# The second MLP product of three batches as seven half-width block products per pair of token blocks

## The chip, the cores and the metric

The kernel runs on one core of a Trainium2 chip. The metric is the device time of one execution in microseconds (us), as the median of several runs. One execution was also recorded by the hardware profiler; its records give the views that are quoted below. Engine names are those of the profile: PE is TensorE's matrix product, PEld its weight load, DVE is VectorE, ACT is ScalarE, POOL is GpSimd, SP is SyncE, which issues the DMAs.

## What is computed

Two blocks in a row, in float32. First an mLSTM cell over 4 batches, 8 heads, 768 time steps and a head size of 40 (a gated linear recurrence; the kernel computes it in chunks of 128 steps). Its output, brought to the shape (4, 768, 320), is `x` of the second block:

```python
X = np.fft.fft(np.fft.fft(x, axis=1), axis=2)
u = x + np.real(X)
un = (u - u.mean(-1)) / np.sqrt(u.var(-1) + 1e-06)
ch = np.maximum(un @ w_ch1, 0.0) @ w_ch2      # 320 -> 1280 -> 320
out = u + ch
```

The change concerns the last product, `relu(...) @ w_ch2`, and the sum with `u`.

## The kernel before

**Order of the work.** The order on every engine is written out by hand. `at(slot, phase, fn, ...)` (L113) puts a function into a plan, `run` (L116) calls all of them in order of slot and phase, and each engine executes its instructions in the order in which they were issued. Within a slot the phases are EVAC (0), FILL (1 and fractions), MAIN (2), FILL_PE (3 and more). MAIN holds the MLP products; FILL holds what DVE, ACT and POOL do for the mLSTM and the Fourier mix of the following batches; FILL_PE holds those batches' PE products, so they come between the MLP products of one slot and those of the next. An engine that waits keeps everything queued behind it waiting as well.

**Tiling.** Tokens come in six blocks of 128 a batch, in the order `ORDER` (L41): three form group 0, three group 1. The hidden features come in ten blocks of 128 (NFF, L27). Batch 0 starts its MLP in slot 31, batches 1, 2 and 3 in slots 63, 95 and 127 (L991 to L995). Each MLP has 20 slots for the first product and 12 for the second.

**First product, batches 1 to 3** (`mlp_block`, L871). Five blocks, each for two hidden feature blocks and both groups (384 tokens each), and each with four steps of one slot. It is already the seven-product scheme: the products accumulate in four PSUM banks p1, p2, p5 and p3, and p1 is read by ACT between two products (L907, L911, L916), so that the next product may add to it. At the end of step 3 DVE adds three banks to the copied values (L921 to L925 by way of L890), POOL applies negated relu to the three results (L893), and ACT takes the fourth straight out of p1 with relu (L927). The next block uses the four banks in reversed order.

**Second product** (`mlp_out`, L929). For each of the six token blocks ten matmuls of 320 columns accumulate in one bank, five in each of two slots (L934). One DVE instruction then multiplies by `rstd`, adds `u` and writes the tile `ot` (L940), and SP stores it (L942).

**Mix.** `mix_seq`, `mix_tail` and `mix_feat` (L636, L649, L700) are its PE products. `mix_add` (L720) adds the transform to `x`, writes the tile `u`, and takes mean and variance (L742, L743): six or eight DVE instructions a token block. `mix_center` (L745, ACT), `mix_turn` (L753, PE) and `mix_turn_out` (L760, ACT) turn it into the first product's operand `uT`. `mlp_sums` (L864) makes four sums of `uT` on DVE ahead of each first product. The mix of batch b+1 lies in the 12 slots of batch b's second product.

**PSUM.** The pool `ps_m` (L82) has four banks that all of these tiles take in rotation. A tile waits until the bank's last reader is done.

Of the kernel before, what the change touches and what calls it, by code (L numbers as in the profile page):

```python
# [19 lines left out]
L = 128  # L20
# [30 lines left out]
def kernel(  # L51
# [25 lines left out]
    xp = pool("xp", 2)  # L77
# [4 lines left out]
    ps_m = pool("ps_m", 4, space=PSUM)  # L82
# [22 lines left out]
    Cd_bufs = [const.tile([L, NP, D1], FP, name=f"Cd{n}") for n in range(2)]  # L105
# [19 lines left out]
    def idle_products(n, ps=ps_s, tag="ps"):  # L125
        pw = ps.tile([L, 2 * L], FP, name="pi", tag=tag)
        for i in range(n):
            nc.tensor.matmul(pw, rest[:, 0:L], rest, start=True, stop=True, skip_group_check=True)


    def gates(gp):
# [19 lines left out]
        idle_products(3, ps_m, "pm")  # L151
# [45 lines left out]
        def spread_max(b, c, h0):  # L197

            k = chunks[b, c]
            if h0 == 0:  # L200
                k.W = wp.tile([L, H, L], FP, name="W", tag="W")
                k.M = []
            k.M.append(ps_m.tile([L, NP, L], FP, name="pM", tag="pm"))
            nc.tensor.matmul(k.M[-1], ident_b, later_b.unsqueeze(1).to_broadcast([L, NP, L]), start=True, stop=False,
                             skip_group_check=True)
            for h in range(h0, h0 + NP):
                bh = b * H + h
                w, x = (ident[:, bh:bh + 1], M[:, c, :]) if c < 2 else (sel[:, bh:bh + 1], M3[:, c, :])
                nc.tensor.matmul(k.M[-1][:, h - h0, :], w.to_broadcast([w.shape[0], L]), x, start=False, stop=True,
                                 skip_group_check=True)  # L210
# [10 lines left out]
        def spread_decay(b, c):  # L221
            k = chunks[b, c]
            k.G = ps_m.tile([L, NP, L], FP, name="pG", tag="pm")
            for h in range(H):
                r, bh = slice(h % 2 * 64, (h % 2 + 1) * 64), b * H + h
                nc.tensor.matmul(k.G[r, h // 2, :], ident[:, bh:bh + 1].to_broadcast([L, 64]), g[:, c, :],
                                 start=True, stop=True)
# [54 lines left out]
        def decays():  # L282
# [4 lines left out]
            pd = ps_m.tile([L, BH // 2, NT - 1], FP, name="pd", tag="pm")  # L287
# [234 lines left out]
    def mlstm_turn(b, c, early):  # L522
        k = chunks[b, c]
        k.px = ps_m.tile([L, NP, L], FP, name="px", tag="pm") if early else ps_h.tile([L, NP, L], FP, name="px", tag="ph")
        for p in range(NP):
            nc.tensor.transpose(k.px[:, p, :], k.hT[:, p, :], ident)  # L526

    def mlstm_finish(b, c):

        k = chunks.pop((b, c))  # L530
        if c == 0:
            xs[b] = xp.tile([L, NT, DM], FP, name="x", tag="x")
# [8 lines left out]
        nc.vector.tensor_tensor(out=xs[b][:, c].rearrange("p (h d) -> p h d", d=D), in0=h1[:, :, 0:D], in1=sc,  # L541
# [41 lines left out]

    def copy(eng, out, in_):
        (nc.scalar.copy if eng == 0 else nc.vector.tensor_copy)(out=out, in_=in_)

    def mix_fold(b, p):
# [3 lines left out]
        x = xs[b]  # L591
# [44 lines left out]
    def mix_seq(b, p, parts):  # L636
# [3 lines left out]
        if p == TG - 1:  # L640
            k.pz = getattr(k, "pz", []) + [ps_m.tile([L, NK], FP, name="pz", tag="pm") for _ in parts]
# [7 lines left out]
    def mix_tail(b, p):  # L649

        k = mixes[b]
        if p == TG - 1:
            k.pzt = ps_m.tile([L, NK], FP, name="pzt", tag="pm")
# [46 lines left out]
    def mix_feat(b, p):  # L700
# [6 lines left out]
        pu = k.pu[p] = ps_m.tile([L, DM + 1 + NC], FP, name="pu", tag="pm")  # L707
# [12 lines left out]
    def mix_add(b, c):  # L720
# [3 lines left out]
        if c == ORDER[0]:  # L724
            k.u = u_p.tile([L, NT, DM + 2], FP, name="u", tag="u")
        ops = (OP.subtract, OP.add) if c >= NT // 2 else (OP.add, OP.subtract)
        u, x, n = k.u[:, c, 0:DM], xs[b][:, c], HALF_D - 1
        pu = k.pu[min(c, NT - 1 - c)]
        P, Q = pu[:, 0:NC], pu[:, NC:DM]
        if b == 0:  # L730
            nc.vector.tensor_tensor(out=u, in0=x, in1=pu[:, 0:DM] if c < TG else backwards(pu, DM, DM), op=OP.add)
        else:
            nc.vector.tensor_tensor(out=u[:, 0:NC], in0=x[:, 0:NC], in1=P, op=OP.add)
            nc.vector.tensor_tensor(out=u[:, NC:], in0=x[:, NC:], in1=backwards(P, n, n), op=OP.add)
            nc.vector.tensor_tensor(out=u[:, 1:HALF_D], in0=u[:, 1:HALF_D], in1=Q, op=ops[0])
            nc.vector.tensor_tensor(out=u[:, NC:], in0=u[:, NC:], in1=backwards(Q, n - 1, n), op=ops[1])
        if c == TG:
            r, own = slice(0, 1), pu[0:1, DM + 1:]
            nc.vector.tensor_tensor(out=u[r, 0:NC], in0=x[r, 0:NC], in1=own, op=OP.add)
            nc.vector.tensor_tensor(out=u[r, NC:], in0=x[r, NC:], in1=backwards(own, n, n), op=OP.add)  # L740
# [12 lines left out]
    def mix_turn(b, c):  # L753

        k = mixes[b]
        pt = k.pt[c] = ps_m.tile([L, 3, L], FP, name="put", tag="pm")
# [56 lines left out]
    def mlp_in(b, gr, f):  # L813
# [4 lines left out]
        if f % 2 == 0:  # L818
            k.pm = [ps_m.tile([L, TG * L], FP, name="pm", tag="pm") for _ in range(2)]
# [7 lines left out]

    def mlp_relu(b, gr, f):
        k = mixes[b]
        if f == 0:  # L830
            k.h[gr] = []
        ht = hT_p.tile([L, TG * L], FP, name="hT", tag="hT")
        nc.scalar.activation(out=ht, in_=k.pm[f % 2], func=AF.Relu, scale=-1.0)  # L833
        k.h[gr].append(ht)
# [36 lines left out]
    def mlp_block(b, i, step):  # L871
# [20 lines left out]
        def relu(h):  # L892
            nc.gpsimd.tensor_scalar(out=h, in0=h, scalar1=-1.0, scalar2=0.0, op0=OP.mult, op1=OP.max)  # L893

        if step == 0:
            if i == 0:
                k.h = {0: [], 1: []}
            banks = [ps_m.tile([L, TG * L], FP, name="pm", tag="pm") for _ in range(4)]
            k.pm = banks[::-1] if i % 2 else banks
            for gr, r in ((0, 0), (1, 0), (0, 1), (1, 1)):  # L900
                k.h[gr].append(hT_p.tile([L, TG * L], FP, name="hT", tag="hT"))
        p1, p2, p5, p3 = k.pm
        (h11, h21), (h12, h22) = k.h[0][f:], k.h[1][f:]
# [13 lines left out]
        else:  # L917
# [4 lines left out]
            relu(h12)  # L922
            add(h22, p5)
            relu(h22)
            add(h11, p2)  # L925
            relu(h11)
            nc.scalar.activation(out=h21, in_=p1, func=AF.Relu, scale=-1.0)  # L927

    def mlp_out(b, gr, i, half):  # L929
        k = mixes[b]  # L930
        if half == 0:
            k.po = ps_m.tile([L, DM], FP, name="po", tag="pm")
        for f in range(half * NFF // 2, (half + 1) * NFF // 2):
            nc.tensor.matmul(k.po, k.h[gr][f][:, i * L:(i + 1) * L], w2_sb[:, f, :], start=(f == 0), stop=(f == NFF - 1))  # L934

    def mlp_store(b, gr, i):
        k = mixes[b]
        c = ORDER[gr * TG + i]
        ot = ot_p.tile([L, DM], FP, name="ot", tag="ot")
        nc.vector.scalar_tensor_tensor(out=ot, in0=k.po, scalar=k.rstd[:, c:c + 1], in1=k.u[:, c, 0:DM],  # L940
                                       op0=OP.mult, op1=OP.add)
        nc.sync.dma_start(out=out[b, c * L:(c + 1) * L, :], in_=ot)  # L942
# [3 lines left out]
    def plan_mlp(b, s):  # L946
        groups = range(NT // TG)
        for i in range(NFF // 2) if b > 0 else ():
            for step in range(4):
                at(s, MAIN, mlp_block, b, i, step)  # L950
                s += 1
        for gr in groups if b == 0 else ():
# [6 lines left out]
        for gr in groups:  # L959
# [11 lines left out]
    def plan_batch(b, s_mlstm, s_mix, s_mlp):  # L971
# [9 lines left out]
        else:  # L981
            feat = [s_mix + 3, s_mix + 4, s_mix + 6]
            add = [s_mix + c for c in (4, 4, 5, 6, 7, 7)]
            turn = [s_mix + c for c in (5, 6, 6)]
            late = [s_mix + c for c in (7, 8, 8)]
# [10 lines left out]
    for n in range(4):  # L996
        at(s_mlp + 2 * NFF + 1 + n, FILL + 0.4, weight_sums, n)

# [26 lines left out]
    u_p = pool("u", 2)  # L1025
    st_p = pool("st", 2)
    hT_p = pool("hT", 2 * NFF)
    ot_p = pool("ot", 2)
# [102 lines left out]
```

## Time and profile before

| what | value |
|---|---|
| median of 3 runs (lowest, highest) | 437.33 us (436.42, 437.35) |
| the profiled execution's own time | 437.06 us |
| its span, first to last instruction | 435.4 us |
| PE busy | 419.1 us, 96% of the span |
| DVE, ACT, POOL busy | 251.6, 169.6, 164.7 us |
| TensorE clock granted | 0.999 |

The time outside the span is 1.7 us. PE's records overlap their neighbours[...]; the pitch from one start to the next is the time it holds the engine. A float32 matmul of the source gives two records in the profile, so 240 matmuls of L934 show as 480. In the groups, the columns are line, engine, operation, tiles (out<-in), shapes and number of records; then busy time in us and mean ns of one; then the idle time of the engine just before these records and what ended it.

Batch 1's second product lies at about 227 to 282 us of the span, batch 2's at 324 to 367 us, batch 3's at 400 to 432 us. Batch 3's has no other batch's work beside it.

### The profile page before, as it was taken

The page shows a single profiled execution, that of the slowest core. Times are in us where ns is not written, and L with a number is a line of the kernel's source. Part 1 is how long each engine was busy: PE and PEld are TensorE (multiplying, and loading weights), DVE is VectorE, ACT ScalarE, POOL GpSimd, SP SyncE. Part 2 cuts the span into 40 slices and gives each one's busy share as a digit, 9 for nine tenths or more (in the row PEclk, how much of TensorE's full clock was granted, in tenths as well). Part 3 has the DMA queues.
Part 4 walks back from the last instruction along what each step waited for, and adds up shares of the span by engine and source line. Part 5 has one row for each costly group of instructions (what it writes and reads, how often), then busy time and mean ns, then how long its engine had stood idle before and what let it go on. Part 6 is the DMA issues. An engine that isn't in the chain of part 4 may idle for free.

```text
span 435.4 us, 7369 instructions
## 1 busy us (share of the span) xinstructions
PE 419.1 (96%) x2696; PEld 284.5 (65%) x2696; DVE 251.6 (58%) x621; ACT 169.6 (39%) x448; POOL 164.7 (38%) x191
## 2 busy tenths in 40 slices
PE   8998999999999999979999999999999999999997
PEld 6877555666577777746457778765457776445774
DVE  8799867689977166587632546667731552343111
ACT  6976376666543114543242334453220131332000
POOL 6454111355424303156682320536681000567000
PEclk9999999999999999999999999999999999999999
DMA  7889396669445424078002334210000000000000
GB/s 245 259 242 336 106 266 221 207 185 280 141 130 160 138 75 150 1 217 206 2 0 87 108 125 131 88 32 3 0 0 17 15 30 32 0 1 2 30 30 30
DMA packets 20547, 47.11 MB, mean 108 GB/s; under 512 B 2784, under 2 KB 9312, under 8 KB 20384
## 3 DMA queue, kind: packets, MB, share of 16 engines
q1 hardware_dynamic: 20512, 46.65, 34.9%
q8 instruction: 21, 0.34, 0.3%
q14 instruction: 14, 0.11, 0.1%
HBM read 42.52 MB, written 4.11 MB: 107 GB/s over the span
## 4 chain that ended last, share of the span: by engine, by line
PE 75%; DVE 14%; DMA 3%; issue 3%; ACT 2%; POOL 1%; SPq 0%; DVEq 0%; POOLq 0%
PE po L934 30%; PE pm L881 13%; PE ps L456 5%; PE ph L477 4%; PE pm L886 3%; PE ph L470 3%; PE pu L718 3%; PE px L526 2%; DMA raw<-in_w 2%; PE pz L687 2%; PE put L758 2%; DMA kvt<-in_kv 1%; PE pz L675 1%; DVE W L462 1%; PE pc L487 1%
## 5 line engine op out<-in xcount | busy, mean ns | idle before, releaser
L934 PE MATMUL po<-w_sb,hT 128*128 128x320 f32 x480 | 135.2, 434 | 0.0
L934 PEld LDWEIGHTS po<-w_sb,hT 128*128 128x128 f32 x480 | 89.6, 190 | 36.9 <-issue 1.4
L893 POOL TENSOR_SCALAR hT<-hT 128x384 f32<-128x384 f32 x45 | 66.3, 1494 | 63.2 <-DVE hT L890 63.2
L434 POOL TENSOR_SCALAR_AFFINE_SELECT W<-W 128x1024 f32<-128x1024 f32 x18 | 21.0, 1166 | 85.3 <-ACT W L412 46.3
L890 DVE TENSOR_TENSOR hT<-hT,pm 128x384 f32<-128x384 f32 x60 | 30.5, 550 | 38.2 <-ACT hT L911 25.7
L940 DVE SCALAR_TENSOR_TENSOR ot<-po,rstd,u 128x320 f32<-128x320 f32 x24 | 13.2, 549 | 67.6 <-PE po L934 67.5
L412 ACT ACTIVATE W<-W,colT 128x128 f32<-128x128 f32 x144 | 45.1, 396 | 0.0
L881 PE MATMUL pm<-uT,w_sb 128*128 128x384 f32 x90 | 32.8, 493 | 3.4 <-DVE hT L890 3.3
L462 DVE TENSOR_TENSOR W<-ps,W 128x512 f32<-128x512 f32 x48 | 30.7, 680 | 7.3 <-POOL W L434 7.0
L822 PE MATMUL pm<-uT,w_sb 128*128 128x384 f32 x80 | 29.9, 500 | 1.1 <-ACT hT L833 0.6
L763 ACT COPY uT<-put 128x384 f32<-128x384 f32 x24 | 10.9, 479 | 48.0 <-PE put L758 48.0
L456 PE MATMUL ps<-qk 40*128 40x128 f32 x384 | 28.1, 284 | 0.0
L456 PEld LDWEIGHTS ps<-qk 40*128 40x128 f32 x384 | 23.7, 187 | 4.4 <-issue 1.0
L477 PE MATMUL ph<-W,kvt 128*41 128x128 f32 x384 | 25.8, 277 | 0.0
L881 PEld LDWEIGHTS pm<-uT,w_sb 128*128 128x128 f32 x90 | 16.0, 190 | 14.9 <-DVE hT L890 7.3
L422 POOL TENSOR_TENSOR qg<-qk,Gb 128x512 f32<-128x512 f32 x18 | 25.5, 1415 | 0.8 <-DMA qk<-in_qkT 0.7
L470 PEld LDWEIGHTS ph<-qg,C 128*128 128x128 f32 x160 | 20.2, 191 | 7.9 <-issue 4.2
L470 PE MATMUL ph<-qg,C 128*128 128x128 f32 x160 | 21.7, 279 | 2.6 <-DVE x L541 1.0
L886 PE MATMUL pm<-uT,w1t_sb 64*128 64x384 f32 x120 | 23.9, 509 | 0.0
L477 PEld LDWEIGHTS ph<-W,kvt 128*41 128x41 f32 x384 | 19.5, 117 | 3.0 <-DVE fe L602 0.2
L515 ACT COPY h<-ph 41x512 f32<-41x512 f32 (+1 forms) x16 | 9.3, 580 | 28.2 <-PE ph L477 28.1
L822 PEld LDWEIGHTS pm<-uT,w_sb 128*128 128x128 f32 x80 | 13.7, 189 | 9.8 <-issue 1.4
(187 smaller groups left out, 643.8 us busy)
## 6 DMA issues: line engine op xcount, KB each, us to landing
W<-M_d SPq DMA_DIRECT2D x18, 512.0 KB
kvt<-in_kv SPq DMA_DIRECT2D x24, 324.0 KB
qk<-in_qkT SPq DMA_DIRECT2D x48, 160.0 KB
raw<-in_w SPq DMA_DIRECT2D x10, 640.0 KB
Gb<-G_d SPq DMA_DIRECT2D x36, 128.0 KB
so<-in_o SPq DMA_DIRECT2D x24, 160.0 KB
out<-ot SPq DMA_DIRECT2D x24, 160.0 KB
ds_sb<-in_dft_s SPq DMA_DIRECT2D x1, 1155.0 KB
```

The source lines that it names most:

```text
L412: nc.scalar.activation(out=k.W[:, h, :], in_=M, func=AF.Exp, scale=-1.0, bias=colT[:, c, 0, b * H + h:b * H + h + 1])
L422: nc.gpsimd.tensor_tensor(out=k.qg, in0=k.qk[:, 0], in1=k.Gb, op=OP.mult)
L456: nc.tensor.matmul(k.ps[hip][:, p, :], k.qk[r, 1, p, :], k.qk[r, 0, p, :], start=True, stop=True)
L462: nc.vector.tensor_tensor(out=Wv, in0=k.ps[hip], in1=Wv, op=OP.mult)
L470: nc.tensor.matmul(k.ph[:, p, :], k.C[:, p, :], k.qg[:, p, :], start=(p == 0), stop=False, skip_group_check=True)
L477: nc.tensor.matmul(k.ph[hip * 64:hip * 64 + D1, p, :], k.v1[:, 2 * p + hip, :], k.W[:, 2 * p + hip, :], start=(c == 0 and p == 0), stop=Tr ...
L822: nc.tensor.matmul(k.pm[i], w1_sb[:, ch, f0:f0 + L], u[2 * ch], start=(ch == 0), stop=False)
L881: nc.tensor.matmul(bank, w, u, start=start, stop=True, skip_group_check=True)
L886: nc.tensor.matmul(bank, block(w1t_sb, i)[rows], mlp_u(gr, 1)[rows], start=False, stop=True, skip_group_check=True)
L890: nc.vector.tensor_tensor(out=h, in0=h, in1=bank, op=OP.add)
L893: nc.gpsimd.tensor_scalar(out=h, in0=h, scalar1=-1.0, scalar2=0.0, op0=OP.mult, op1=OP.max)
L934: nc.tensor.matmul(k.po, k.h[gr][f][:, i * L:(i + 1) * L], w2_sb[:, f, :], start=(f == 0), stop=(f == NFF - 1))
```

## The change

Batch 0 keeps its second product. Batches 1 to 3 get another one. One token block of group 1 and one of group 0 form a pair, the ten hidden blocks fall into five even and five odd ones, and the 320 output columns into two halves of 160. This is a 2 by 2 by 2 block product, and `mlp_out_pair` does it with seven block products of five matmuls of 160 columns, in four slots: two products in steps 0, 1 and 2, one in step 3. The two PSUM banks x and y are used in turns. After every block product one DVE instruction (`residual`) adds the bank's present content, times `rstd`, to one half of one token block of `u`; x then goes on accumulating on what was read.

The scheme needs sums of operands. Four sums of weights (`out_weight_sums`) are made once, on POOL. Four sums of hidden values (`hidden_sums`) are made for each pair. For pair 0 POOL makes them for four fifths of the features, two slots ahead of the end of the first product, and DVE makes the last fifth at the head of the first slot of the second product; for pairs 1 and 2 DVE makes S1 and S3 and POOL S2 and S4, in the two last slots of the pair before.

Further parts: the three relus of each first-product block go from POOL to ACT (`mlp_relus`), in EVAC of the slot after step 3. `u` is no longer a tile of its own: `mix_add` and `residual` work in place on `x`, which is kept in two fixed buffers, and the store reads from there. The PSUM pool has four tags of one bank. Where no bank is named they rotate as before; the pairs use banks 0 and 1, and the mix of batches 2 and 3 banks 2 and 3. Of the mix of batches 2 and 3, the third feature product, two adds and four turns come one or two slots later. A token block's store is issued in MAIN, right after its last `residual`, where it stood in EVAC of the next slot; and `mlstm_finish` (L528), which fills `x` of batch b+2, now waits for the stores of batch b.

```diff
-            nc.tensor.matmul(k.po, k.h[gr][f][:, i * L:(i + 1) * L], w2_sb[:, f, :], start=(f == 0), stop=(f == NFF - 1))
...
+    MIX = {"z": (2, 3), "zt": 2, "u": (3, 2, 2), "ut": (3, 3, 3, 3, 2, 3)}
...
-        def relu(h):
-            nc.gpsimd.tensor_scalar(out=h, in0=h, scalar1=-1.0, scalar2=0.0, op0=OP.mult, op1=OP.max)
...
+            k.pm = [bank("pm", [L, TG * L], n) for n in (range(4) if i % 2 else range(3, -1, -1))]
...
             add(h12, p3)
-            relu(h12)
             add(h22, p5)
-            relu(h22)
             add(h11, p2)
-            relu(h11)
             nc.scalar.activation(out=h21, in_=p1, func=AF.Relu, scale=-1.0)
 
+    def mlp_relus(i):
+        for gr, r in ((1, 1), (1, 0), (0, 0)):
+            h = hidden(gr, 2 * i + r)
+            nc.scalar.activation(out=h, in_=h, func=AF.Relu, scale=-1.0)
+
+    def residual(b, c, cols, po):
+        k = mixes[b]
+        u = k.u[:, c, cols]
+        nc.vector.scalar_tensor_tensor(out=u, in0=po, scalar=k.rstd[:, c:c + 1], in1=u, op0=OP.mult, op1=OP.add)
...
+    MLP_PAIRS = ((0, 1), (2, 0), (1, 2))
...
+    def out_weight_sums(n):
...
+        nc.gpsimd.tensor_tensor(out=o, in0=x, in1=y, op=OP.subtract)
...
+    def hidden_sums(eng, n, which, f0=0, f1=NFF // 2):
...
+        for j in which:
+            o, x, y, op = ((S1, A21, A22, OP.add), (S2, S1, A11, OP.subtract), (S3, A11, A21, OP.subtract),
+                           (S4, A12, S2, OP.subtract))[j - 1]
+            eng.tensor_tensor(out=o, in0=x, in1=y, op=op)
+
+    def mlp_out_pair(b, n, step):
...
+        if step == 0:
+            k.po = [bank("po", [L, HALF_D], (n + j) % 2) for j in range(2)]
...
+        def product(po, a, w, start=False):
+            for f in range(half):
+                nc.tensor.matmul(po, a[:, f], w[:, f], start=start and f == 0, stop=f == half - 1, skip_group_check=True)
...
+        if step == 0:
+            product(x, pair_block(n, 1, 1), w[0, 0], True)
+            residual(b, c1, first, x)
+            product(y, pair_block(n, 1, 0), w[1, 0], True)
+            residual(b, c1, first, y)
+        elif step == 1:
+            product(x, s(2), w2x["T2"])
+            residual(b, c1, last, x)
+            product(y, s(1), w[0, 1], True)
+            residual(b, c2, last, y)
+        elif step == 2:
+            product(x, s(3), w2x["T3"])
+            residual(b, c2, last, x)
+            product(y, s(4), w[1, 1])
+            residual(b, c1, last, y)
+            store(b, c1)
+        else:
+            product(x, pair_block(n, 0, 0), w2x["T4"])
+            residual(b, c2, first, x)
+            store(b, c2)
...
                 at(s, MAIN, mlp_block, b, i, step)
                 s += 1
+            at(s, EVAC, mlp_relus, i)
...
+        if b > 0:
+            at(s - 2, FILL + 0.3, hidden_sums, nc.gpsimd, 0, (1, 2, 3, 4), 0, NFF // 2 - 1)
+            at(s, EVAC, hidden_sums, nc.vector, 0, (1, 2, 3, 4), NFF // 2 - 1, NFF // 2)
+        for n in range(TG) if b > 0 else ():
+            for step in range(4):
+                at(s, MAIN, mlp_out_pair, b, n, step)
+                if n < TG - 1 and step > 1:
+                    for eng, j in ((nc.vector, 2 * step - 3), (nc.gpsimd, 2 * step - 2)):
+                        at(s, FILL + 0.3, hidden_sums, eng, n + 1, (j,))
+                s += 1
...
+            feat = [s_mix + c for c in ((3, 4, 6) if b == 1 else (3, 4, 7))]
+            add = [s_mix + c for c in ((4, 4, 5, 6, 7, 7) if b == 1 else (4, 4, 5, 6, 8, 8))]
+            turn = [s_mix + c for c in ((5, 6, 6) if b == 1 else (5, 6, 7))]
+            late = [s_mix + c for c in ((7, 8, 8) if b == 1 else (8, 9, 10))]
...
+        at(s_mlp + MLP_SLOTS + 3 + 3 * n, FILL + 0.4, out_weight_sums, n)
```

## The prediction, made before the changed kernel was run

> **What bounds the kernel now.** I read the page first: engine shares, then the chain that ended last.
>
> ```profile
> PE 419.1 (96%) x2696; PEld 284.5 (65%) x2696; DVE 251.6 (58%) x621; ACT 169.6 (39%) x448; POOL 164.7 (38%) x191
> PE 75%; DVE 14%; DMA 3%; issue 3%; ACT 2%; POOL 1%; SPq 0%; DVEq 0%; POOLq 0%
> ```
>
> PE is the bound, and three quarters of the chain are its own. Then the groups that the change touches, and the busy time by stage (batch 1's second product, batch 2's first, batch 2's second, batch 3's first, batch 3's second; columns: stretch, length, then busy us of PE, PEld, DVE, ACT, POOL).
>
> ```profile
> L934 PE MATMUL po<-w_sb,hT 128*128 128x320 f32 x480 | 135.2, 434 | 0.0
> L893 POOL TENSOR_SCALAR hT<-hT 128x384 f32<-128x384 f32 x45 | 66.3, 1494 | 63.2 <-DVE hT L890 63.2
> L940 DVE SCALAR_TENSOR_TENSOR ot<-po,rstd,u 128x320 f32<-128x320 f32 x24 | 13.2, 549 | 67.6 <-PE po L934 67.5
> ...
> 226.00:282.50 56.50, 56.50 (x406) 43.62 (x408) 26.49 (x74) 21.23 (x60) 20.08 (x24) 1.00 0.32 104
> 282.50:324.00 41.50, 39.85 (x231) 23.84 (x228) 27.03 (x78) 14.48 (x35) 24.01 (x25) 1.00 0.03 9
> 324.00:367.00 43.00, 43.00 (x190) 30.99 (x190) 16.30 (x50) 7.30 (x15) 4.26 (x3) 1.00 0.06 20
> 367.00:399.60 32.60, 32.50 (x112) 16.51 (x111) 12.35 (x34) 9.15 (x19) 18.22 (x13) 1.00 0.02 5
> ```
>
> In the second-product stages PE never rests and no other engine is busy half the time. So time saved on PE there is saved in full, unless a new wait appears. Where would one? Two places in the timeline. First, a boundary between two blocks of batch 3's first product (start, length, instruction, idle before it):
>
> ```profile
> 379.36 0.91 PE L881 MATMUL pm<-m,w_sb 128*128 128x384 f32 x2
> 380.11 2.10 PE L881 MATMUL pm<-uT,w_sb 128*128 128x384 f32 x6
> 382.05 0.81 PE L881 MATMUL pm<-raw 128*128 128x384 f32 x2
> ...
> 380.31 0.49 ACT L927 ACTIVATE hT<-pm 128x384 f32<-128x384 f32 x1 [1.84 <-PE pm L881]
> 381.01 0.48 ACT L907 COPY hT<-pm 128x384 f32<-128x384 f32 x1 [0.21 <-POOL hT L893]
> ```
>
> PE's new block starts at 380.11; the product at 382.05 adds to p1 and needs L907's copy, done at 381.49. ACT has 0.56 us to spare. Second, the pitch of narrow matmuls and DVE's lumps in batch 1's second product:
>
> ```profile
> 244.57 0.71 PE L718 MATMUL pu<-dd_sb,Z 128*128 128x161 f32 x4
> 245.12 0.70 PE L718 MATMUL pu<-dd_sb,Zt 128*128 128x320 f32 x2
> ...
> 245.86 0.32 DVE L733 TENSOR_TENSOR u<-x,pu 128x161 f32<-128x161 f32 x1 [0.53 <-PE pu L718]
> 249.17 1.27 DVE L462 TENSOR_TENSOR W<-ps,W 128x512 f32<-128x512 f32 x2
> ```
>
> Four records of about 160 columns take 245.12 - 244.57 = 0.55 us, 0.136 each (the same pair at 248.35 and 248.89 gives 0.135). From 245.86 DVE does two `mix_add` (3.3 us) and one weighing (1.27), 4.6 us without a break.
>
> [...] L934's pitch is 32.31 us for 120 records in the chain, 0.269 us[...]. For 160 it gives 0.136, as measured on L718; weight loads of 128 columns stay hidden at that pitch there. [...] L869 took 0.56 us alone and 1.32 beside POOL. [...]
>
> **What the change takes away.** Per batch, 120 records of 0.269 (32.3 us) become 3 pairs x 35 matmuls x 2 records = 210 of 0.136 (28.6 us). Over three batches: 96.9 - 85.7 = 11.2 us. The last residual is half as wide: 0.549 less 160 columns at the slope between L731 (320 columns, 0.474) and L733 (161, 0.309), so 0.38; it ends the kernel, 0.17 saved. Sum 11.4. POOL loses 45 relus, 66 us, off the path: no gain counted.
>
> **What it adds on the path.**
>
> *Relus on ACT.* Each is queued ahead of the next block's L907. Consecutive ACT instructions overlap by 0.10 (L412: 144 of 0.396 busy 45.1, a pitch of 0.313), so three take 3 x 0.42. From L927 at 380.31: relus start at 380.70, 381.12 and 381.54, L907 at 381.96, done 382.44. PE starts 0.06 later and its first weight load shows (0.1; such a record takes 0.42 instead of 0.32): 382.60 for 382.05, 0.55 us lost. Batch 3 has four such boundaries: 2.2. In batches 1 and 2 the first two are covered by another batch's product between the blocks or by PE's own wait for DVE, the third is late by about 0.4 (ACT waits there for DVE's adds, which end 0.9 us after PE's restart), the fourth has no cover: 0.95 a batch. Sum 4.1. Bounds: 0.48 a relu (L520, 320 columns) gives 3.2, 0.61 (L751, with a bias operand) gives 6.1. Exponentials queued behind the relus have a slot to spare.
>
> *Into the second product.* DVE's four last sums (128 elements, about 0.28 + wait, 1.3 us) wait for ACT's third relu, and the residual of x is queued behind them. In batch 3: relus end 2.1 us after PE's start, sums 3.4, residual 3.75, and PE wants x again at 2.72: 0.85 to 1.0, with 0.15 before it for the fifth matmul, which waits for a relu. In batch 2 the mix product (1.37) covers all but 0.15; in batch 1 scores (1.09) and mix cover all. Sum 1.15 (0.5 to 1.6).
>
> *Residuals behind DVE's lumps.* PE needs a bank back one product (1.36 us) later; bare residual and waits take 0.7, so nothing is lost until something stands before it on DVE. In batch 1, slot 87: the lump (4.6), then 0.38 + 0.06 + 0.1, against PE's 2.72 + 1.08 - 0.16 = 3.64: 1.5 lost. In batch 2, slot 119, without weighing: 0.3. Slot 121 (add, S1): 0.2. Slot 123: third pair of adds 3.85 (it handles its own first row too), against 0.33 + 2.72 + 0.33 - 0.16 = 3.22: 1.1. Elsewhere the mLSTM's 3.4 us on PE hide the lump; gone, they would cost 1 to 2 each. Sum 3.1 (1.5 to 4.5).
>
> *mlp_sums.* Now behind the last residual. Between batches 1 and 2 the mLSTM hides it. Between 2 and 3 the second sum is ready 1.75 after PE's end, wanted at 1.29: 0.5 (0 to 0.8).
>
> *S1 to S4.* DVE 0.82 each (L859, 640 elements); POOL about 1.7 (L422, 1.415 for 512), a pair ahead of use. Where S3 and POOL's S4 contend in batch 3, the residual behind S3 is late: 0.5 (0 to 1.5).
>
> At nothing: POOL's weight sums (some 8 us, where it had 22 us of relus), in-place adds (same instructions), banks 2 and 3 for the mix (each tile's reader ends a slot earlier). Stores stay last on the same queue; loads behind them have five slots. `mlstm_finish` waits for stores: the tightest, issued at 185.8, is wanted at 191.6, and the last store of all needed 2.7 to the end. If it took over 6, DVE would stop there.
>
> Sum: -11.4 + 4.1 + 1.15 + 3.1 + 0.5 + 0.5 = -2.0. The profiled execution (span 435.4, 437.06 in all) becomes 435.0; the median lies 0.27 higher: 435.3, rounded down for less contention once POOL's relus are gone: 435.1.
>
> **Rivals.** *Slack absorbs the waits*: the low ends (3.2, 0.5, 1.5, 0, 0) add 5.2: 437.3 - 11.4 + 5.2 = 431.1. For it: DVE is busy less than half of these stages. Against: the lumps are queued in order. *The waits eat the gain*: 11.4 against 11: 437. For it: each bank returns with only 0.6 us to spare. *Slower: the first weight load of each block product shows*, since a product's first matmul waits for DVE: 63 products x 0.1 = 6.3 on top: 435.1 + 6.3 = 441.4. It decides above 0.05 us a product. For it: every restart after a wait shows it, as at 382.6 above. Against: L881 waits for DVE at many starts that keep 0.323. *Not doing what it says*: excluded, the issued order has 105 matmuls of 160 columns a batch for 60 of 320.
>
> **Chances.** Likeliest (433 to 436.3) 0.44; slack 0.24; eaten 0.15; slower, by weight loads or stalls I do not see, 0.17. The likeliest case reaches a little over the line, and the eaten case spreads to both sides. A measurement tells about 0.2% from no change, 436.45 to 438.2. Faster 0.68, same 0.14, slower 0.18. Range 431.0 to 438.8: the low ends below; above, the middle of the high ends (6.1 + 1.6 + 4.5 + 0.8 + 1.5 = 14.5, 440.4), which leaves out some 0.17.
>
> **What would show it.** Pitch 0.136 on the 630 new records, about 86 us. ACT's relu near 0.52, and PE idle before the product after the p1 copy, 0.5 each in batch 3. PE waits ended by DVE's residual, 1.5 in batch 1 and 1.6 in batch 2. Wrong if the pitch is above 0.15, or if waits ended by residuals sum to over 6 us.

## The result and the profile after

The changed kernel takes 443.92 us (median of 4 runs, 443.22 to 444.40) beside 437.34 us for the kernel before on the same chip: a ratio of 1.0152 (95% interval 1.013 to 1.0174), slower by 6.6 us where 2 us less had been predicted. The profiled execution took 443.22 us with a span of 441.5 us, 6.1 longer than before. In the four groups of runs of this document the kernel before had medians of 437.34, 437.74, 437.48 and 437.84 us, so a difference between experiments of different groups is uncertain by some 0.5 us.

First the busy time of each engine, the chain that ended last by engine, and three groups: DVE's adds of the first product (L907, L890 before), its residuals (L951) and PE's block products (L1000; one of several groups of that line).

```profile
PE 416.4 (94%) x2966; PEld 303.5 (69%) x2966; DVE 281.9 (64%) x690; ACT 187.7 (43%) x493; POOL 141.7 (32%) x174
...
PE 70%; DVE 17%; ACT 5%; issue 4%; DMA 1%; POOL 1%; ACTq 0%; DVEq 0%; POOLq 0%
...
L907 DVE TENSOR_TENSOR h<-h,pm 128x384 f32<-128x384 f32 x60 | 30.5, 550 | 41.1 <-ACT h L920 28.5
L951 DVE SCALAR_TENSOR_TENSOR x<-po,rstd,x 128x160 f32<-128x160 f32 (+1 forms) x69 | 27.2, 395 | 45.7 <-PE po L1000 37.9
...
L1000 PE MATMUL po<-T,S 128*128 128x160 f32 x180 | 27.7, 301 | 2.7 <-DVE x L951 2.6
```

PE is busy 2.7 us less than before, and its share of the chain fell from 75 to 70%: the time is lost in PE's waits, and (below) at a lower clock (0.988 granted for 0.999). Where do the waits lie? PE's waits, by its line and by the line that ended them (us in total, times, longest):

```profile
PE pm L898 <- DVE h L907: 4.7, 4, 2.5
PE pm L898 <- DVE x L951: 3.6, 1, 3.6
PE po L1000 <- DVE x L951: 2.6, 3, 1.3
PE pm L838 <- ACT e L353: 2.0, 1, 2.0
PE put L774 <- ACT uc L767: 1.7, 5, 0.4
```

Only the third line is a wait of the new product. The largest single one, 3.6 us, is that of a *first* product (L898) for a residual (L951). The stages tell the same. Each length runs from PE's first MLP record of a stage to that of the next (the first row: from the start of the span); the last two columns are experiments 5 and 8 below.

| stage | before | after | difference | banks as before | sums late |
|---|---|---|---|---|---|
| up to batch 0's MLP | 57.40 | 59.39 | +1.99 | 58.50 | 58.36 |
| batch 0, first product | 65.44 | 66.23 | +0.79 | 64.70 | 64.97 |
| batch 0, second (not changed) | 58.58 | 58.58 | 0 | 58.58 | 58.58 |
| batch 1, first | 45.59 | 51.60 | +6.01 | 46.80 | 45.31 |
| batch 1, second (new) | 56.26 | 55.29 | -0.97 | 55.28 | 55.29 |
| batch 2, first | 41.24 | 41.72 | +0.48 | 41.74 | 40.94 |
| batch 2, second (new) | 42.74 | 40.67 | -2.07 | 40.68 | 40.68 |
| batch 3, first | 32.43 | 34.73 | +2.30 | 34.74 | 32.91 |
| batch 3, second (new) | 35.69 | 33.28 | -2.41 | 33.30 | 33.29 |

The three new products gain 5.45 us, and 8.8 are lost before the first of them begins. Three places make most of the 8.8 (the relus' share in batch 1 comes with experiment 4).

**A: PE waits before batch 0's first MLP product.** PE's and then DVE's timeline (start, length, instruction, idle before it and what ended it), first of the kernel before, then of the changed one:

```profile
57.40 2.85 PE L822 MATMUL pm<-uT,w_sb 128*128 128x384 f32 x8
...
58.67 0.48 DVE L731 TENSOR_TENSOR u<-x,pu 128x320 f32<-128x320 f32 x1
```

```profile
56.77 0.60 PE L139 MATMUL pi<-rest 128*128 128x256 f32 x2
59.39 0.98 PE L838 MATMUL pm<-uT,w_sb 128*128 128x384 f32 x1 [2.03 <-ACT e L353]
```

```profile
58.37 0.48 DVE L348 TENSOR_SCALAR m<-raw 128x640 uint32<-128x640 uint32 x1
58.77 0.48 DVE L751 TENSOR_TENSOR x<-x,pu 128x320 f32<-128x320 f32 x1
59.28 0.49 DVE L758 BATCH_NORM_STATS2 stats<-x 128x6 f32<-128x320 f32 x1
```

The profile names ACT, but this matmul also waits for DVE in the program, and it starts 0.14 us after DVE's `mix_add` (L751) is done with its bank `pu`. Before, the first product did not wait for that add: it began 1.27 us ahead of it. The banks in the two programs, by physical number:

```
                                    before                after
batch 0: pu tiles of mix_feat       7, 4                  7, 4
         put tiles of mix_turn      6, 5, 7               5, 6, 7
         first MLP tile             6 (a put, long read)  4 (the second pu, read by mix_add in slot 31)
batch 1: batch 0's last po          6                     6
         first block p1, p2, p5, p3 4, 7, 5, 6            7, 6, 5, 4
```

So the pool of four did not rotate, as the section on the change has it ("they rotate as before"): its order (6, 5, 7 for the three `put`, then 6 again) is no rotation, and fits a pool that gives the bank that came free first. The tags of one bank do rotate, and the turn falls on a bank that isn't free.

**B: batch 1's first product.** PE and DVE of the kernel before, then PE and DVE of the changed one:

```profile
181.42 1.46 PE L881 MATMUL pm<-uT,w_sb 128*128 128x384 f32 x4
...
185.21 0.54 DVE L940 SCALAR_TENSOR_TENSOR ot<-po,rstd,u 128x320 f32<-128x320 f32 x1
```

```profile
184.21 0.81 PE L898 MATMUL pm<-uT,w_sb 128*128 128x384 f32 x2
188.60 1.38 PE L898 MATMUL pm<-uT,w_sb 128*128 128x384 f32 x2 [3.58 <-DVE x L951]
```

```profile
186.75 1.32 DVE L886 TENSOR_TENSOR m<-uT,raw 128x384 f32<-128x384 f32 x1
188.00 0.54 DVE L951 SCALAR_TENSOR_TENSOR x<-po,rstd,x 128x320 f32<-128x320 f32 x1
```

The product into p2 waits for the residual of batch 0's last token block, since p2 now has that block's bank. The residual's product was done at 180.27, but on DVE it stands behind `mlp_sums` (L886, from 184.97, after 4.84 us of waiting for ScalarE's `uT`); it starts 3.79 us after the stage's first product, exactly as it did before; there the bank was p3's, wanted last, and the products into p1 and p2 ran on.

**C: the first fold of batch 2** (the mix's sums and differences of tiles of `x`). DVE and PE of the kernel before:

```profile
193.72 0.49 DVE L595 TENSOR_TENSOR eo<-x 128x320 f32<-128x320 f32 x1
...
196.04 1.56 PE L881 MATMUL pm<-uT,w_sb 128*128 128x384 f32 x4 [0.82 <-DVE hT L890]
```

DVE, then POOL, then PE of the changed one:

```profile
198.77 2.21 DVE L608 TENSOR_TENSOR eo<-x 128x320 f32<-128x320 f32 x1
...
202.20 1.48 DVE L907 TENSOR_TENSOR h<-h,pm 128x384 f32<-128x384 f32 x3
```

```profile
198.75 1.87 POOL L972 TENSOR_TENSOR T<-w_sb 128x800 f32<-128x800 f32 x1
```

```profile
202.81 1.65 PE L898 MATMUL pm<-uT,w_sb 128*128 128x384 f32 x2 [2.53 <-DVE h L907]
```

POOL's weight sum began 0.02 us before the fold, whose two operands lie in SBUF. The fold took 2.21 us (0.49 before, and in experiment 3 without that overlap); the adds of h, in order behind it, and PE behind the adds were late. The prediction had seen L869 take 1.32 us beside POOL for 0.56, and counted on less contention without POOL's relus (a fold of before took 0.78 us for 0.49 beside one, at 207.21 us); it didn't apply this to the weight sums. The adds from PSUM (L907) keep 0.5 us each: three take 1.48 us from 202.20, with POOL's next weight sum beside them from 202.85.

**The clock.** After each of the three gaps TensorE runs at half clock (0.50 in the record of the clock). Windows of the trace: pairs of the stretch before and the stretch of half clock (stretch, length, busy us of PE, PEld, DVE, ACT, POOL, granted clock, DMA share, GB/s):

```profile
55.78:59.19 3.41, 1.39 (x7) 0.58 (x6) 3.34 (x6) 2.10 (x4) 0.00 (x0) 1.00 1.04 283
59.40:62.80 3.40, 3.40 (x6) 1.94 (x7) 2.83 (x5) 1.71 (x5) 0.00 (x0) 0.53 1.04 243
185.49:188.90 3.41, 0.30 (x1) 0.30 (x2) 3.27 (x7) 1.83 (x6) 2.72 (x2) 1.00 0.00 0
189.00:192.40 3.40, 3.40 (x9) 2.08 (x8) 2.82 (x8) 0.00 (x0) 1.10 (x3) 0.51 0.71 217
199.14:202.55 3.41, 1.14 (x4) 0.30 (x2) 3.31 (x6) 0.49 (x1) 2.16 (x3) 1.00 0.85 214
202.50:206.00 3.50, 3.19 (x7) 1.88 (x8) 2.38 (x5) 1.72 (x4) 3.42 (x4) 0.51 0.69 227
```

Each lasts 3.413 us in the trace's record of the clock; half of that, 1.7 us, is an estimate of the most that it can cost by itself. The kernel before has none between 4.3 us and 434.4 us of its span. The three stretches begin at 59.20, 188.91 and 202.56 us, 38 and 4 times 3.413 us apart: in this trace they lie on one grid of windows of 3.413 us.

### The profile page after: what moved, and what is told of

Same layout as the page of the kernel before. It is cut to its first block, busy times and chain, and to the rows that moved or that the text cites. A ratio compares the mean times of both kernels' runs of the same rounds, so it can differ in the third digit from the quotient of the medians.

```text
span 441.5 us, 8027 instructions
## 1 busy us (share of the span) xinstructions
PE 416.4 (94%) x2966; PEld 303.5 (69%) x2966; DVE 281.9 (64%) x690; ACT 187.7 (43%) x493; POOL 141.7 (32%) x174
## 4 chain that ended last, share of the span: by engine, by line
PE 70%; DVE 17%; ACT 5%; issue 4%; DMA 1%; POOL 1%; ACTq 0%; DVEq 0%; POOLq 0%
PE po L1000 16%; PE pm L898 12%; PE po L945 7%; PE ps L467 5%; PE ph L488 4%; PE pu L731 3%; PE pm L903 3%; PE ph L481 3%; PE pm L838 3%; PE px L537 2%; ACT h L938 2%; PE pz L700 2%; PE put L774 2%; DMA kvt<-in_kv 1%; PE pz L688 1%
## 5 line engine op out<-in xcount | busy, mean ns | idle before, releaser
L907 DVE TENSOR_TENSOR h<-h,pm 128x384 f32<-128x384 f32 x60 | 30.5, 550 | 41.1 <-ACT h L920 28.5
L951 DVE SCALAR_TENSOR_TENSOR x<-po,rstd,x 128x160 f32<-128x160 f32 (+1 forms) x69 | 27.2, 395 | 45.7 <-PE po L1000 37.9
L898 PE MATMUL pm<-uT,w_sb 128*128 128x384 f32 x90 | 35.8, 526 | 8.6 <-DVE h L907 4.7
L945 PE MATMUL po<-w_sb,h 128*128 128x320 f32 x120 | 34.4, 435 | 0.0
L838 PE MATMUL pm<-uT,w_sb 128*128 128x384 f32 x80 | 31.2, 521 | 2.5 <-ACT e L353 2.0
L473 DVE TENSOR_TENSOR W<-ps,W 128x512 f32<-128x512 f32 x48 | 30.6, 679 | 2.6 <-POOL W L445 2.4
L898 PEld LDWEIGHTS pm<-uT,w_sb 128*128 128x128 f32 x90 | 16.6, 199 | 21.0 <-DVE h L907 8.5
L1000 PE MATMUL po<-T,S 128*128 128x160 f32 x180 | 27.7, 301 | 2.7 <-DVE x L951 2.6
L945 PEld LDWEIGHTS po<-w_sb,h 128*128 128x128 f32 x120 | 22.2, 190 | 9.5 <-issue 0.8
L1000 PEld LDWEIGHTS po<-T,S 128*128 128x128 f32 x180 | 25.4, 190 | 4.6 <-issue 4.0
L1000 PE MATMUL po<-w_sb,h 128*128 128x160 f32 x180 | 26.9, 302 | 0.2
L1000 PEld LDWEIGHTS po<-w_sb,h 128*128 128x128 f32 x180 | 25.2, 190 | 2.0 <-DVE x L951 0.7
L986 POOL TENSOR_TENSOR S<-S,h 128x640 f32<-128x640 f32 (+1 forms) x9 | 13.1, 1456 | 41.7 <-DVE S L986 25.6
```

What stands on the lines that cost most here:

```text
L473: nc.vector.tensor_tensor(out=Wv, in0=k.ps[hip], in1=Wv, op=OP.mult)
L838: nc.tensor.matmul(k.pm[i], w1_sb[:, ch, f0:f0 + L], u[2 * ch], start=(ch == 0), stop=False)
L898: nc.tensor.matmul(bank, w, u, start=start, stop=True, skip_group_check=True)
L907: nc.vector.tensor_tensor(out=h, in0=h, in1=bank, op=OP.add)
L945: nc.tensor.matmul(k.po, hidden(gr, f)[:, i * L:(i + 1) * L], w2_sb[:, f, :], start=(f == 0), stop=(f == NFF - 1))
L951: nc.vector.scalar_tensor_tensor(out=u, in0=po, scalar=k.rstd[:, c:c + 1], in1=u, op0=OP.mult, op1=OP.add)
```

## The experiments

Two theories stood against each other. *Upstream*: the turn of the banks, POOL's sums and the half clock, all ahead of the new product, make the loss. *Own waits* (the rival, and what the prediction feared): the residuals and relus of the new product are worse than priced. Each edit is to the changed kernel unless it says otherwise; times are medians, ratios to the kernel before with 95% intervals.

**1. Another bank for batch 0's first tile.**

```diff
+        if (gr, f) == (0, 0):
+            turn[0] += 1
```

(The tiles of the last slots ahead of batch 1 were named, so that B stays.)

> One edit to the changed kernel: the turn of the four PSUM banks is moved on by one ahead of batch 0's first MLP product, so that its first tile doesn't fall on a bank that a late mix_add still reads (the last tiles before batch 1's first product keep the banks they have now). Upstream theory (the loss lies ahead of the new product: banks, POOL beside DVE, and the half clock after each gap): the 2.03 us before the first L838 go, the 3.4 us of half clock behind it too, batch 1 starts 2.8 us earlier, and the kernel takes 441.1 us (440.4 to 442.0). Rival (the loss is the new product's own waits, its residuals and relus; what is earlier upstream is lost again there): 443.4 to 443.9 us.

Measured 442.03 us, 1.0102 (1.0064 to 1.014): 1.9 less, just above the range that was expected. PE's wait for L353 is gone and in the profiled execution the clock stays whole there; but 11 us on a 1.6 us wait for a relu (L854) appears. The third pair of tiles gets the banks of the second pair, as it does in the changed kernel; there PE came late enough not to notice. So it is shown that the bank makes the wait of A, and also that another rotation is no cure: with banks as the pool gave them (experiment 5) this wait is absent too. What A costs is not shown here. In the profiled execution batch 1 starts at 184.35 us for 184.21: the 0.90 gained at the start is lost again, 0.16 in batch 0's first product, with its new wait, and 0.89 in its second, whose last bank this edit names. The gain lies in batch 1's first product (49.85 us for 51.60), where the half clock behind C is missing though C's gap of 2.5 us is there; experiment 6 shows such a case. The four runs spread from 440.17 us (granted clock 1.000) to 444.31 (0.992).

**2. Another bank for batch 0's last `po`.**

```diff
-            k.po = bank("po", [L, DM])
+            k.po = bank("po", [L, DM], LAST_PO if (gr, i) == (1, TG - 1) else None)
```

(LAST_PO is 0; the last three transposes of batch 1's mix get banks 2, 3, 1.)

> One edit to the changed kernel: the second product of batch 0's last token block and the last three transposes of batch 1's mix take other banks, so that the bank of that product is wanted last (as p3) and not second (as p2) by batch 1's first block. Upstream theory: PE's stall of 3.7 us at the start of batch 1's first product falls to about 1.1 as in the kernel before, and the half clock behind it goes: 3 us less in all, 440.9 us (440.0 to 442.3). Rival (own waits of the new product): 443.4 to 443.9 us.

Measured 439.27 us, 1.0041 (1.0026 to 1.0055): 4.7 less, more than expected. Batch 1's first product takes 46.41 us for 51.60 (and batch 0's second 0.9 more, for the renamed bank); the trace has no 3.6 us wait, and of the three stretches of half clock only the one behind A. Without the stall the fold meets POOL's sum for a shorter time (1.21 us for 2.21), so part of C goes too (PE's longest wait for the add of h: 1.5 for 2.5). The own-waits theory, which gave 443.4 to 443.9, fails.

**3. POOL's weight sums ahead of the fold.**

```diff
-        at(s_mlp + MLP_SLOTS + 3 + 3 * n, FILL + 0.4, out_weight_sums, n)
+        at(s_mlp + MLP_SLOTS + (1, 1, 1, 12)[n], FILL + 0.4, out_weight_sums, n)
```

> One edit to the changed kernel: POOL's first three weight sums for the second product are put two slots and more ahead of batch 2's first fold, where POOL idles. Upstream theory (POOL's sum makes DVE's fold of two SBUF operands slow, and DVE's adds and PE's next product wait behind it): the fold takes 0.5 us again instead of 2.21, PE's wait for the add of h falls from 2.5 to 1 or less, no half clock there, 2.5 to 3.5 us less in all: 440.4 to 441.4 us. Rival: the add is late because PE stalled 3.7 us earlier, not because of POOL; then the fold is faster, and the kernel stays within 0.6 us of 443.9.

Measured 440.92 us, 1.0071 (1.0056 to 1.0086): 3.0 less. The fold takes 0.49 us, PE's longest wait for the add falls to 0.8, the half clock behind C is gone, B's wait of 3.6 and its half clock stay. C is shown as a cause of its own, given B.

**4. Relus behind the next block's first copy.**

```diff
-            at(s, EVAC, mlp_relus, i)
+            at(s, FILL_PE + 8 if i < NFF // 2 - 1 else EVAC, mlp_relus, i)
```

> One edit to the changed kernel: ScalarE's three relus of a block are issued behind the next block's first copy, except those of the last block. If the relus ahead of that copy cost what was predicted (0.55 at each of four boundaries in batch 3, 0.95 in each of batches 1 and 2), batch 3's first product takes 32.5 us for 34.7 and the whole 2.2 to 4.1 us less: 439.8 to 441.7 us. If batch 3's first product is longer for another reason (contention on SBUF, say), it stays at 34.7 and the kernel at 443.9 us within 0.6.

Measured 440.33 us, 1.0067 (1.0048 to 1.0085): 3.6 less. Batch 3's first product takes 32.91 us for 34.73, batch 2's 40.94 for 41.72, batch 1's 50.84 for 51.60. ScalarE at the same boundary, first of the changed kernel, then of this one:

```profile
380.67 0.49 ACT L933 ACTIVATE h<-pm 128x384 f32<-128x384 f32 x1 [1.85 <-PE pm L898]
381.06 1.34 ACT L938 ACTIVATE h<-h 128x384 f32<-128x384 f32 x3
382.30 0.47 ACT L916 COPY h<-pm 128x384 f32<-128x384 f32 x1
```

```profile
378.94 0.49 ACT L933 ACTIVATE h<-pm 128x384 f32<-128x384 f32 x1 [1.85 <-PE pm L898]
379.59 0.48 ACT L916 COPY h<-pm 128x384 f32<-128x384 f32 x1 [0.15 <-PE pm L898]
379.96 1.35 ACT L938 ACTIVATE h<-h 128x384 f32<-128x384 f32 x3
```

The three relus take 1.34 us either way; only their place in the queue cost time.

**5. Banks as the pool gave them.** From batch 0's first MLP tile to batch 1's mix, a table in place of the turn (renamed so that batch 1's block keeps its order):

```diff
+    BANKS = (0, 1, 2, 3, 0, 1, 0, 2, 3, 1, 3, 0, 2, 0, 1, 3, 2, 0, 1, 3, 2, 0, 1, 3,
+             2, 0, 1, 3, 2, 0, 1, 2, 3, 0, 2, 1, 3, 2, 0, 3, 2, 1)
...
+        if n is None and GIVEN:
+            n = GIVEN.pop(0)
```

> The changed kernel with the banks alone put back: from batch 0's first MLP product to batch 1's mix they are those which the pool of four gave in the kernel before, by a table. Bank theory: both waits go (before batch 0's first product, and PE's 3.6 us for the residual of batch 0's last block), with the half clock behind each: batch 0's stages as in the kernel before, batch 1's first product 46 us for 51.6, in all 436.8 us (436 to 438). If the fixed turn of banks is not the cause, no more than the sum of the two runs that moved single tiles can't be reached either: 438 to 444 us.

Measured 436.02 us, 0.9962 (0.9949 to 0.9975): 7.9 less, now ahead of the kernel before. The record of the clock has it whole from 7.3 us to 433.9 of 434.3 us. By stages it is 0.89 less up to batch 0's MLP, 1.53 in batch 0's first product and 4.80 in batch 1's. Batch 1's start, on PE:

```profile
181.78 1.46 PE L905 MATMUL pm<-uT,w_sb 128*128 128x384 f32 x4
184.20 0.66 PE L540 MATMUL px<-ident,h 128*128 128x128 f32 x4 [0.97 <-ACT h L529]
184.70 0.81 PE L905 MATMUL pm<-uT,w_sb 128*128 128x384 f32 x2
```

Both first products of the block run, and p5's follows after 0.97 us of an mLSTM wait, as it did before. The banks alone turn the sign.

**6. Filling the gap, twice.** Does the half clock cost by itself? Seven idle products in gap B, first in a bank of the scores.

```diff
             product(p1, A[0, 0], mlp_u(0, 0), True)
+            if (b, i) == (1, 0):
+                idle_products(7)
             product(p2, A[0, 1], mlp_u(0, 2), True)
```

> The changed kernel with seven idle products (0.43 us each, into a bank of their own) put on PE in the gap of 3.7 us at the start of batch 1's first product, between the products into p1 and p2; nothing is taken out. Clock theory (a gap of this length costs a second time, since the clock is halved for 3.4 us behind it): the stall stays, the half clock behind it goes, and the stage takes 0.8 to 1.7 us less: 442.2 to 443.1 us. If the half clock costs nothing that the later wait for the add of h wouldn't cost anyway: 443.9 us within 0.5.

Measured 449.02 us, 1.0273 (1.0249 to 1.0297): 5.1 more. The filler itself waited 5.0 us for the scores' reader (L473), so this says nothing of the clock. Again, in p5's bank:

```diff
             product(p1, A[0, 0], mlp_u(0, 0), True)
+            for _ in range(7 if (b, i) == (1, 0) else 0):
+                product(p5[:, 0:2 * L], rest[:, 0:L], rest, True)
             product(p2, A[0, 1], mlp_u(0, 2), True)
```

> The changed kernel with seven idle products in the gap at the start of batch 1's first product again, this time written to p5's bank, which is free there and is started anew afterwards (the first form of this waited 5 us for a bank of the scores, so that it made a gap of its own). Clock theory: the stall for the residual stays, the half clock of 3.4 us behind it goes, the stage takes 0.8 to 1.7 us less than 51.6: 442.2 to 443.1 us. Rival (the later wait for the add of h takes back what the full clock gives): 443.9 us within 0.5.

Measured 440.98 us, 1.0061 (1.0037 to 1.0084): 2.9 less, more than expected, though PE only does more. The stall is as long as in the changed kernel: from the first product to p2's 4.39 us (185.29, not shown, to 189.68; 184.21 to 188.60 above). PE's timeline there:

```profile
186.08 3.29 PE L898 MATMUL pm<-rest 128*128 128x256 f32 x14
189.68 0.91 PE L898 MATMUL pm<-uT,w_sb 128*128 128x384 f32 x2 [0.31 <-DVE x L953]
...
202.20 1.56 PE L898 MATMUL pm<-uT,w_sb 128*128 128x384 f32 x4 [2.53 <-DVE h L907]
```

The stage falls by 3.2 us for *two* stretches of half clock. From its start to the product behind C it takes 16.91 us for 18.60 (184.21 to 202.81 above), so 1.7 go with the stretch behind B; 1.5 go after it, with the stretch behind C, although C's gap of 2.53 us is still there. Two windows of this run, around C's gap:

```profile
198.00:201.40 3.40, 1.67 (x8) 0.49 (x4) 3.30 (x6) 0.59 (x2) 2.16 (x3) 1.00 0.95 260
201.40:204.80 3.40, 2.60 (x11) 1.75 (x12) 3.30 (x9) 1.72 (x4) 3.32 (x5) 1.00 0.93 229
```

On a grid of 3.413 us from this run's one stretch of half clock, behind A, the gap now falls across the border of two windows, with PE busy 1.67 and 2.60 us; the changed kernel had 1.14 in one window ahead of its half clock. So by these records the second half of this gain is the grid's phase, which the filler didn't set out to move; the first half, 1.7 us, is the second price of B.

**7. Three causes mended at once** (table, sums early, relus later).

> The changed kernel with all three causes mended at once: from batch 0's first MLP product to batch 1's mix the banks are those which the pool of four gave in the kernel before (a table), POOL's first three weight sums lie ahead of the fold, and the relus of a block lie behind the next block's first copy. If the causes are separate and what they cost adds up (banks some 7 of the stages seen so far, sums 3.0, relus 3.6): 443.9 - 13.6 = 430.3 us (429.5 to 433). If one wait hid another, so that the same microseconds were counted twice: 433 to 437 us.

Measured 434.51 us, 0.9933 (0.9907 to 0.9959): 4.2 above the 430.3 of the sum, so causes overlap. Batch 1's first product takes 47.26 us, 0.5 *more* than with the table alone. DVE, then POOL:

```profile
188.46 1.48 DVE L553 SCALAR_TENSOR_TENSOR so<-so,den 128x320 f32<-128x320 f32 x1
...
194.97 1.45 DVE L613 TENSOR_TENSOR eo<-x 128x320 f32<-128x320 f32 x1
```

```profile
187.70 1.89 POOL L979 TENSOR_TENSOR T<-w_sb 128x800 f32<-128x800 f32 x1
...
194.80 1.27 POOL L436 TENSOR_TENSOR qg<-qk,Gb 128x512 f32<-128x512 f32 x1
```

Early, the sums meet `mlstm_finish` (L553, 1.48 for 0.49), and push POOL's own scaling (L436, done at 193.08 with the table alone) onto the fold (L613).

**8. The same with the sums late**, all four in slot 75, behind a POOL instruction that waits for DVE's second fold.

```diff
+        at(s_mlp + MLP_SLOTS + 12, FILL + 0.6, out_weight_sums, n)
```

> Banks by the table and relus behind the copy as in the run with all mended, but POOL's four weight sums all wait for slot 75, where they stand behind a POOL instruction that waits for the second fold, and so run when batch 2's folds and finishes are done. Contention theory (where the sums run beside a DVE instruction of two SBUF operands, that one takes 1.0 to 1.7 us longer; early, they met mlstm_finish instead of the fold and pushed POOL's own mLSTM work onto the fold): batch 1's first product takes 44.5 to 45.5 us, for 47.3 with the sums early and 46.8 with the banks alone; the kernel 431.5 us (430.8 to 432.5). Rival (the sums are not what makes DVE late there; it is the order of the adds behind the mLSTM's work): the stage stays at 46 or more, the kernel at 433 to 434.5 us.

Measured 432.09 us, 0.9873 (0.9858 to 0.9889). Batch 1's first product takes 45.31 us, within the 44.5 to 45.5 expected. Of the 1.5 us against the table alone, the sums make 0.7 if the relus make the 0.76 that they made in experiment 4: with the banks right, C is small.

**9. The old second product in the mended kernel.** Experiment 7 with 60 matmuls of 320 columns a batch for batches 1 to 3, whole residuals, and no sums.

```diff
-        for n in range(TG) if b > 0 else ():
-            for step in range(4):
-                at(s, MAIN, mlp_out_pair, b, n, step)
...
-        for gr in groups if b == 0 else ():
+        for gr in groups:
```

> The kernel with all three causes mended, but with batches 1 to 3's second product as in the kernel before (60 matmuls of 320 columns a batch, no sums of weights or hidden values, whole residuals). It measures the new product by itself, by the difference to the run with all mended. By the sums of the prediction (11.4 gained, 5.25 given back by waits for residuals and sums): the old product is 6.2 us slower, some 436.5 us if the mended kernel takes 430.3. Rival (the new product's own waits eat its gain): within 1 us of the mended kernel.

Measured 437.82 us, 1.0008 (0.9998 to 1.0019): 3.3 above experiment 7, and 5.7 above experiment 8, where the sums are out of the way. The prediction's sums gave 6.15. By stages, against experiment 8, batches 1 to 3's second products gain 2.30, 2.06 and 2.40, and batch 3's first product loses 0.58: 6.2. The new product is worth what was predicted.

**10. Adds behind the residuals** (experiment 8, and batches 2 and 3's `mix_add` behind the products of their slot).

```diff
-            at(a, FILL, mix_add, b, c)
+            at(a, FILL if b < 2 else FILL_PE + 7, mix_add, b, c)
```

> The run with sums late, and batches 2 and 3's mix_adds moved behind the block products of their slot on VectorE, so that the residuals no longer stand behind a lump of adds. Lump theory, as predicted (a residual behind adds and weighing holds PE's bank back, 1.5 us in batch 1 and 1.6 in batch 2): PE's waits for residuals fall from 2.6 us to under 1, 1.5 to 2.5 us less: 429.5 us (428.8 to 430.5) if the run with sums late takes 431.5. Rival (the adds are then late for the mix's own transposes, and PE waits for those instead): no gain, or up to 1 us more.

Measured 431.01 us, 0.9843 (0.9826 to 0.986): 1.1 less than experiment 8, not the 1.5 to 2.5 expected. PE's waits for residuals in the new product:

```profile
PE po L1007 <- DVE x L958: 0.8, 2, 0.4
```

They were 2.6. Batch 1's second product takes 53.78 us for 55.29, the 1.5 that the prediction had for its lump; batch 2's takes 40.92 for 40.68. There the residual's wait of 0.98 falls to 0.40, but a transpose of the mix now waits for the moved adds:

```profile
357.02 0.52 PE L779 MATMUL put<-ident,uc 128*128 128x128 f32 x3 [0.73 <-DVE x L761]
```

So in batch 2 the rival of this experiment came true. This is the fastest version seen.

## Why the prediction was wrong

**The gain held.** Twenty records of 160 columns take 2.72 us, 0.136 each. Batch 3's second product fell by 2.41 us; the prediction's terms for it (3.74 and 0.17 gained, 1.0 and 0.5 given back) make 2.41. That this is exact is luck: the starts that come later than 0.136 after the one before sum to 0.77 at the head of the stage (for 1.0) and 0.75 further on (for 0.5).

**The relus held.** 4.1 predicted, 3.6 won back by moving them (by stages 0.76, 0.78 and 1.82 for 0.95, 0.95 and 2.2), with a relu at 0.513 us for 0.52 and 0.412 from start to start for 0.42. The 0.52 was the author's estimate; the trace of before showed only its bounds, 0.48 and 0.61. The last block of each batch stays in the queue. The 0.5 for `mlp_sums` between batches 2 and 3 held as well (0.58, experiment 9).

**The residuals held in the main.** Waits of L1000 for L951 sum to 2.6 us, below the 6 named as the sign of error: 1.26 in batch 1 for the 1.5 predicted, 0.98 in batch 2 for 1.6, and 0.37 at the head of batch 3, which belongs to another term. Not foreseen were 1.2 us in batch 1: two transposes now wait. ScalarE, then PE at the first of them:

```profile
267.64 0.61 ACT L767 ACTIVATE uc<-x 128x384 f32<-128x384 f32 x1
```

```profile
268.31 0.55 PE L774 MATMUL put<-ident,uc 128*128 128x128 f32 x3 [0.43 <-ACT uc L767]
```

PE idles 0.43 and 0.42 us there; from start to start the matmul before takes 0.73, 0.59 over its pitch of 0.136. They wait for the mix's centring (L767), queued behind the mLSTM's copies on ACT. Experiment 9, with the old product but the moved mix slots, has the same two waits (0.61 each over the pitch), and the kernel before has not. So it is not the new product that costs this, and most likely the moved slots, for which the prediction had no term; slots moved back alone were not measured.

**What failed is the list "At nothing".** "POOL's weight sums (some 8 us, where it had 22 us of relus)" counted POOL's time and not where it falls: beside a fold, which it made 1.7 us longer on the path to PE. Moving them won 3.0 us in the changed kernel (experiment 3), but only some 0.7 with the banks right (experiment 8). And "banks 2 and 3 for the mix (each tile's reader ends a slot earlier)" looked at the tiles with a named bank alone. The tiles *without* one, of batch 0 and of batch 1's mix, were taken to lie where they lay, because the diff seemed only to rename the pool. That step cost 7.9 us (experiment 5), more than the whole loss of 6.6. By stages: 0.89 up to batch 0's MLP; 1.53 in batch 0's first product, where the half clock behind A lies; and 4.80 in batch 1's, with B's wait of 3.6 (of which 1.0 is waited elsewhere when B goes), the half clock behind B and C, and a part of the meeting of sum and fold, which B's delay made longer (2.21 us for 1.20 in experiment 5). It could be read before the run from the two programs' bank numbers.

**The rivals.** The slower one had the right side and the wrong mechanism: of the 63 block products 38 start directly behind another one, and 35 of these starts keep the pitch (under 0.16 us, where it needed 0.05 more a product). Of the other 25, which start behind other work, the trace can't tell. Its side remark, "stalls I do not see", is what came.

**Open.** The split of the 7.9 us among its parts is not exact: experiments 1 and 2 overlap with C, and the time of PE's first MLP record differs by 0.8 us among the experiments with the same table (57.7 to 58.5), so that the 0.89 of A's wait is hardly more than this spread. A and its half clock together stand out more clearly: batch 0's second product starts at 125.63 us, for 122.6 to 123.3 with the table.

## What to carry to other kernels

When a pool of buffers becomes named or rotating ones, list for each tile which tile's reader holds its bank, in both programs: an allocation is part of the schedule. Work that an idle engine takes over has a place as well as a length; ask which instruction runs beside it, and who waits for that one. And price a gap on TensorE twice where a stretch of half clock follows it in the record: behind B's wait of 3.6 us that was 1.7 us more (experiment 6).

## What the runs showed of the hardware

In the changed kernel, stretches of half clock of 3.413 us followed gaps of 2.03 and 2.53 us, shorter than themselves. What went with the half clock is PE's busy time in the window of the grid ahead of it. On the changed kernel's grid, from 4.6 us of its span on, half clock follows the windows at whole clock with PE busy 1.39, 0.30, 1.14 and, at the kernel's end, 0.37 us, and no others; of the others the least busy has 2.15. Between these, other runs show both. Two windows, of experiment 2 (followed by half clock) and of experiment 7 (not):

```profile
55.40:58.81 3.41, 1.63 (x9) 0.82 (x7) 3.34 (x7) 1.93 (x4) 0.00 (x0) 1.00 1.03 281
187.19:190.60 3.41, 1.41 (x6) 0.54 (x5) 3.27 (x8) 2.19 (x7) 3.25 (x3) 1.00 0.74 218
```

The 1.67 us of experiment 6 had none behind it either. So these records give a range and no exact threshold. And where the grid lies went with it: the same gap of 2.53 us cost a stretch of half clock in the changed kernel and none in the second run of experiment 6.
